# The six-expert part of a mixture-of-experts kernel: VectorE's and ScalarE's order written by hand, background work put into named slots

## Chip, core and metric

The kernel runs on one core of one Trainium2 chip. The metric is the device time of one execution in microseconds (us), taken as the median of several runs. TensorE multiplies matrices, VectorE (DVE in the profile) and ScalarE (ACT) do elementwise work, SyncE (SP) issues the transfers (DMA), GpSimd (POOL) has next to nothing to do here.

## The reference

A gated linear recurrence over 4 sequences of 768 positions gives `x` with 3072 rows (tokens) of 384 numbers. On it works a dense mixture of 8 experts, whose gate is normalised by 8 alternating row and column passes (Sinkhorn):

```python
P = np.exp(logits - logits.max())
for _ in range(8):
    P /= P.sum(1, keepdims=True) + 1e-09
    P /= P.sum(0, keepdims=True) + 1e-09
    P *= N / E
out = 0
for e in range(8):
    h = np.maximum(x @ w1[e], 0.0)      # 384 -> 1024
    out += P[:, e:e + 1] * (h @ w2[e])  # 1024 -> 384
```

Every expert is applied to every token, in float32.

## The kernel before

The first part computes the recurrence and, beside it, experts 0 and 1, whose outputs go to DRAM (`ye_d`). A short middle part (`phase2a`) loads the first tokens of the second part, prepares two sets of weights and does three of the eight normalisations. The rest is the six-expert part (`phase2b`), which the change concerns.

**Steps.** The tokens are four units of 768, taken two at a time (`su`, and `ul` within it). For each `su`, each expert `e` from 2 to 7, each of the two units and each of the four pairs `p` of 128-wide feature blocks there is a step: 96 steps, numbered `n` from 0. Within an expert's eight steps I write `q = 4*ul + p`. In n, an expert starts at 0, 8, 16, ..., the second pair of units at 48.

**Numbers.** Every float32 factor is split into a high and a low part, and a product takes three matmuls (high x high, high x low, low x high). "Hi" is a copy on ScalarE, "lo" a subtraction on VectorE.

**A step's first layer** computes a 2 x 2 grid of blocks (two feature blocks, two halves of 384 tokens) by Strassen's scheme with seven products P1 to P7 (`prod`, matmuls of lines 784 to 786) from weight sums S1 to S5 and token sums T1 to T4. P1, P6 and P7 have one term (3 matmuls each); P5, P2, P4 and P3 have two (6 each), as the third block of channels is added there. The products live in two PSUM banks (`psA`). ScalarE copies P1 to `s1` and P5 to `s5`; VectorE adds u2 = P6 + s1, u3 = P7 + u2, u4 = u2 + s5, c22 = u3 + s5, c11 = P2 + s1, c21 = P4 + u3, c12 = P3 + u4 (`add`, line 794). A product's bank is free when its copy or sum is done. `relu` then makes the hidden block's high half on ScalarE (line 805) and its low half on VectorE (line 806). With the product these are named h11, h00, h10, h01 for c22, c11, c21, c12.

**A step's second layer** works on the hidden blocks of the step before (`prev`): six groups of six matmuls, one for each tile of 128 tokens, `l2(0)` to `l2(5)` (here G0 to G5, `second`, lines 745 to 747). They gather over the four pairs of an expert in six PSUM banks. After the fourth pair VectorE adds the bank, weighted by the gate, to an accumulator `oa` in SBUF (line 754; for expert 2 ScalarE copies it, line 752), and after expert 7 the accumulator is written out.

**Background work** beside the steps:
- `raw_w` (line 647) loads raw weights; `prep_w` makes from them the five sums S1 to S5 (line 665) and, by ScalarE copies and VectorE subtractions (lines 667, 668), the tiles `wa`, `wb` (first layer) and `wc` (second layer). Twelve tiles of one expert fill the ring `wp`; the next expert's can be made only as these fall free.
- `load_x` (line 618) loads another unit's tokens; its jobs (lines 622 to 626) make T1 to T4.
- `rows` and `columns` do one normalisation of P.
- `start` (lines 729 to 733) loads the outputs of experts 0 and 1 for a tile, multiplies the accumulator by the gate and adds both.

**Order.** TensorE's order is written by hand: the build records its instructions in program order inside `tc.manual_schedule`. The order on VectorE, ScalarE and SP is found by the framework's scheduler when the kernel is built, from simulated times; each engine then runs its queue strictly in that order, and a DMA issue that waits holds the issues behind it on SP. In program order, background work stands in `l2` (two jobs a time), behind G1 and G4 (`rows`, `columns`), and behind G5 (`prep_w`, `start`). TensorE's order within a step is P1, P6, G0, P7, G1, P5, G2, P2, G3, P4, G4, P3, G5.

Of the kernel before, what the change touches and what calls it, by code (L numbers as in the profile page):

```python
# [13 lines left out]
H, D = 8, 48  # L14
# [40 lines left out]
class Net:  # L55
# [550 lines left out]
    def load_x(self, pool, ul, u):  # L606
        nc, V = self.nc, self.nc.vector
# [11 lines left out]
        jobs = []  # L619

        def job(o, a, b, op=ALU.subtract):
            jobs.append(lambda: V.tensor_tensor(o, a, b, op))

        def split(nm, r):
            jobs.append(lambda: nc.scalar.activation(X[nm][:, 0], r, AF.Copy))
            jobs.append(lambda: V.tensor_tensor(X[nm][:, 1], r, f(nm, 0), ALU.subtract))

        job(t[0], f("B11", 0), f("B11", 1), ALU.add)
        job(t[1], t[1], t[4], ALU.add)
        job(t[0], t[1], t[0])  # L630
        split("T1", t[0])
        job(t[2], f("B22", 0), f("B22", 1), ALU.add)
        job(t[3], t[2], t[0])
        split("T2", t[3])
        job(t[1], t[2], t[1])
        split("T3", t[1])
        job(t[2], f("B21", 0), f("B21", 1), ALU.add)
        job(t[2], t[2], t[3])
        split("T4", t[2])
        return jobs  # L640

    def raw_w(self):
        if self.nraw == len(self.todo):
            return
        e, p = self.todo[self.nraw]
        raw = self.wr.tile([128, 2, 2 * C], F32, tag="raw", name=f"raw{self.nraw}")
        self.nc.sync.dma_start(raw, self.w[e, 2 * p:2 * p + 2].rearrange("f p c -> p f c"))
        self.raw[self.nraw] = raw
        self.nraw += 1

    def prep_w(self):
        nc, V, A = self.nc, self.nc.vector, self.nc.scalar
        n = self.nprep
        if n == len(self.todo):
            return
        self.nprep += 1
        raw = self.raw.pop(n)
# [4 lines left out]
        w2 = self.wp.tile([128, 2, 2, C], F32R, tag="w", name=f"wc{n}")  # L662
        A11, A12, A13, A21, A22, A23 = (R[:, i, c] for i in range(2) for c in range(3))
        for o, a, b, op in ((0, A21, A22, ALU.add), (1, s[:, 0], A11, ALU.subtract), (2, A11, A21, ALU.subtract), (3, A12, s[:, 1], ALU.subtract), (4, A13, A23, ALU.subtract)):
            V.tensor_tensor(s[:, o], a, b, op)
        for t, k, src in ((wa, slice(0, 3), R[:, 0, :3]), (wa, slice(3, 5), R[:, 1, 1:3]), (wb, slice(0, 5), s), (w2, slice(0, 2), raw[:, :, C:])):
            A.activation(t[:, 0, k], src, AF.Copy)
            V.tensor_tensor(t[:, 1, k], src, t[:, 0, k].bitcast(F32), ALU.subtract)
        W = {nm: (wa, k) for k, nm in enumerate(("A11", "A12", "A13", "A22", "A23"))}
        W.update({f"S{k + 1}": (wb, k) for k in range(5)})  # L670
        self.W[n] = (W, w2)
        self.raw_w()

    def phase2a(self, c2):
# [8 lines left out]
        self.nraw = self.nprep = 0  # L683
# [14 lines left out]
        for k in range(HEAD):  # L698
            self.rows()
            more(3)  # L700
            self.columns(self.psK.tile([128, E], F32, tag="po", name=f"cp{k}"))
            if k == 1:
                self.raw_w()
                self.prep_w()
                self.prep_w()
# [3 lines left out]
    def phase2b(self, c2):  # L709
        tc, nc = self.tc, self.nc  # L710
        self.hp = c2.enter_context(tc.tile_pool(name="hp2", bufs=2))
        xb = c2.enter_context(tc.tile_pool(name="xb", bufs=1))
        psD = c2.enter_context(tc.tile_pool(name="psD", bufs=2, space=bass.MemoryType.PSUM))
        steps = [(su, e, ul, p) for su in range(SU) for e in range(2, E) for ul in range(SU) for p in range(NF // 2)]
        npair = NF // 2
        po, oa, H = {}, {}, {}
# [8 lines left out]
        def start(u, k):  # L725
            tt = tile_of(u, k)
            y = [self.wr.tile([128, C], F32, tag="y", name=f"y{q}_{tt}", bufs=4) for q in range(2)]
            for q in range(2):
                nc.sync.dma_start(y[q], self.ye_d[q][tt])
            o = oa[tt]  # L730
            nc.vector.tensor_scalar(o, o, self.P[:, tt, 2:3], None, ALU.mult)
            for q in range(2):
                nc.vector.scalar_tensor_tensor(o, y[q], self.P[:, tt, q:q + 1], o, ALU.mult, ALU.add)

        def second(st, k):
            su, e, ul, p = st
            u = su * SU + ul
            h, w2 = H[st]
            if p == 0:
# [8 lines left out]
            if p == npair - 1:  # L748
                tt = tile_of(u, k)
                if e == 2:  # L750
                    oa[tt] = self.xa.tile([128, C], F32, tag=f"oa{u % SU}_{k}", name=f"oa{tt}")
                    nc.scalar.activation(oa[tt], po[k], AF.Copy)
                else:
                    nc.vector.scalar_tensor_tensor(oa[tt], po[k], self.P[:, tt, e:e + 1], oa[tt], ALU.mult, ALU.add)
                if e == E - 1:
                    nc.sync.dma_start(self.out[tt * CH:tt * CH + CH, :], oa[tt])

        V, A = nc.vector, nc.scalar
        jobs, free = [], [(pool, tag) for pool, tag in ((self.psC, "po0"), (self.psC, "po1"), (self.psC, "po2"), (psD, "po"), (psD, "po"))]
        it = HEAD  # L760
        for n, st in enumerate(steps + [None]):
            prev = steps[n - 1] if n else None
            if st is None:
                for k in range(2 * NS):
                    second(prev, k)
                break
            su, e, ul, p = st
            u = su * SU + ul
            if e == 2 and ul == 0 and p == 1:
                jobs = self.load_x(xb, 1, u + 1)  # L770
            if e == E - 1 and ul == 1 and p == 1 and su + 1 < SU:
                jobs = self.load_x(self.xa, 0, u + 1)
            W, w2 = self.W[(su * (E - 2) + e - 2) * npair + p]
            X = self.X[u]
            h = {}
            H[st] = (h, w2)

            def prod(nm, *terms):
                pool, tag = free.pop(0) if n == 0 and nm not in ("P1", "P6") else (self.psA, "ph")
                ps = pool.tile([128, TH], F32, tag=tag, name=f"{nm}_{n}")  # L780
                for q, (wn, xn) in enumerate(terms):
                    (t, k), x = W[wn], X[xn]
                    first, last = q == 0, q == len(terms) - 1
# [18 lines left out]
            def relu(i, j, c):  # L802
                hh = self.hp.tile([128, TH], F32R, tag=f"hh{i}{j}", name=f"hh{i}{j}_{n}")
                hl = self.hp.tile([128, TH], F32R, tag=f"hl{i}{j}", name=f"hl{i}{j}_{n}")
                A.activation(hh, c, AF.Relu)  # L805
# [3 lines left out]
            def l2(k):  # L809
                if prev is not None:  # L810
                    second(prev, k)
                if p > 1 or n == 0 or su and e == 2:
                    for _ in range(min(2, len(jobs))):
                        jobs.pop(0)()
                if k == 1 and 0 < n <= ITERS - it:
                    self.rows()
                if k == 4 and 0 < n <= ITERS - it:
                    self.columns(self.psA.tile([128, E], F32, tag="ph", name=f"cp{it + n - 1}"))

            s1 = copy("s1", prod("P1", ("A11", "B11")))  # L820
            u2 = add("u2", prod("P6", ("S2", "T2")), s1)
            l2(0)
            u3 = add("u3", prod("P7", ("S3", "T3")), u2)
            l2(1)
# [19 lines left out]
            if e == 3:  # L844
                a = p * 2 if ul == 0 else 8 + p
                for k in range(a, a + 2 - ul):
                    start(su * SU + k // (2 * NS), k % (2 * NS))
# [174 lines left out]
```

## Time and profile before

| | |
|---|---|
| median of 3 runs | 1842.44 us (1840.32 to 1843.8) |
| span of the profiled execution, first to last instruction | 1839.6 us |
| six-expert part in it, P1 of step 0 to the last group's last matmul | 663.6 to 1833.7 us |
| TensorE, its weight loads, VectorE, ScalarE busy | 96%, 94%, 74%, 40% of the span |
| TensorE's granted clock, mean over the span | 0.988 |

The profiled execution has no time other than its span; what a run's time has beyond it lies ahead of the first and behind the last instruction. In the profile, PE is TensorE's matmul row and PEld the weight loads that run ahead of it. Matmuls overlap in their records (each of 384 columns is given 0.334 us, and the next starts 0.173 later), so a busy PE is not a sign of peak speed; a gap between starts, and what ended it, is what to read. A row of waits gives the waiting engine, its tile and line, the engine and line that released it, and then the total, the count and the longest in us. A row of groups gives line, engine, operation, tiles and shapes, the count, busy us and mean ns of one, and the idle time before them. A row by stretches gives the stretch, its length, then busy us and count of PE, PEld, DVE, ACT and POOL, the clock, the DMA's share and GB/s.

### The profile page before, as it was taken

The numbers are of one execution on the slowest core, as the hardware profiler recorded it, in microseconds if no ns is written. First come the engines' busy times: TensorE is split into PE (matmuls) and PEld (weight loads), VectorE is DVE, ScalarE is ACT, GpSimd is POOL, SyncE is SP. The second block draws the span as 40 slices with busy tenths as digits, with TensorE's granted clock in tenths as the row PEclk, the third lists the DMA queues.
The fourth block names the chain that finished last, engine by engine and source line by source line (L and its number), as shares of the span: only waits on it lengthen the run. The fifth ranks groups of instructions, "written<-read, shape, count | busy, mean of one in ns | idle before, by whom it ended". The sixth has DMA issues, their size and how long they took to land.

```text
span 1839.6 us, 30590 instructions
## 1 busy us (share of the span) xinstructions
PE 1774.3 (96%) x12024; PEld 1731.9 (94%) x12024; DVE 1361.8 (74%) x3060; ACT 734.3 (40%) x1597; POOL 6.4 (0%) x15
## 2 busy tenths in 40 slices
PE   5979999999999999999999999999999999999998
PEld 3869999999999989899999999998999999999998
DVE  7888989888883586967676767687776767575754
ACT  7534444445443443424242424343433333242421
POOL 1000000000000000000000000000000000000000
PEclk9979999999999999999999999999999999999999
DMA  6333433333332430401010101123220101020100
GB/s 209 96 104 88 132 113 110 116 111 111 118 97 73 147 112 4 150 20 52 18 52 18 52 18 52 49 96 97 69 86 18 52 5 65 1 69 1 52 24 31
DMA packets 120632, 132.83 MB, mean 72 GB/s; under 512 B 9632, under 2 KB 100512, under 8 KB 120480
## 3 DMA queue, kind: packets, MB, share of 16 engines
q1 hardware_dynamic: 119680, 130.41, 23.0%
q8 instruction: 96, 1.57, 0.4%
q14 instruction: 56, 0.46, 0.1%
q10 hardware_dynamic: 800, 0.39, 0.1%
HBM read 88.22 MB, written 23.59 MB: 61 GB/s over the span
## 4 chain that ended last, share of the span: by engine, by line
PE 82%; DVE 9%; DMA 4%; ACT 2%; issue 1%; SPq 1%; DVEq 0%; ACTq 0%
PE po L747 10%; PE po L745 10%; PE po L746 10%; PE P L784 9%; PE P L785 9%; PE P L786 9%; PE po L158 3%; PE ph L180 3%; PE ph L181 3%; PE ph L179 3%; PE po L160 3%; PE po L159 3%; PE sp L474 2%; PE y L491 2%; DMA raw<-in_w_dram 2%; PE U L469 1%
## 5 line engine op out<-in xcount | busy, mean ns | idle before, releaser
L747 PE MATMUL po<-wc,hl 128*128 128x384 f32 x1152 | 385.3, 334 | 3.1 <-DVE hl L806 3.1
L745 PE MATMUL po<-wc,hh 128*128 128x384 f32 x1152 | 385.0, 334 | 0.0
L746 PE MATMUL po<-wc,hh 128*128 128x384 f32 x1152 | 384.8, 334 | 0.0
L805 ACT ACTIVATE hh<-c 128x384 fp32r<-128x384 f32 x384 | 200.9, 524 | 322.2 <-DVE c L794 320.9
L806 DVE SCALAR_TENSOR_TENSOR hl<-c,hh 128x384 fp32r<-128x384 f32 x384 | 211.9, 552 | 66.5 <-ACT hh L805 58.5
L747 PEld LDWEIGHTS po<-wc,hl 128*128 128x128 f32 x1152 | 216.2, 188 | 4.4 <-DVE hl L806 4.4
L745 PEld LDWEIGHTS po<-wc,hh 128*128 128x128 f32 x1152 | 216.2, 188 | 0.4 <-ACT hh L805 0.4
L746 PEld LDWEIGHTS po<-wc,hh 128*128 128x128 f32 x1152 | 216.2, 188 | 0.0
L799 ACT ACTIVATE s<-P 128x384 f32<-128x384 f32 x192 | 94.1, 490 | 270.8 <-PE P L786 270.8
L185 ACT ACTIVATE hh<-ph 128x256 fp32r<-128x256 f32 x192 | 73.3, 382 | 243.7 <-PE ph L181 243.0
L180 PE MATMUL ph<-xl,w 128*128 128x256 f32 x576 | 162.8, 283 | 5.4 <-DVE xl L531 5.4
L179 PE MATMUL ph<-xh,w 128*128 128x256 f32 x576 | 162.2, 282 | 0.6 <-ACT xh L530 0.6
L181 PE MATMUL ph<-xh,w 128*128 128x256 f32 x576 | 162.4, 282 | 0.0
L784 PE MATMUL P<-B,wa 128*128 128x384 f32 x480 | 160.7, 335 | 0.9 <-DVE c L794 0.6
L786 PE MATMUL P<-B,wa 128*128 128x384 f32 x480 | 160.4, 334 | 0.0
L785 PE MATMUL P<-B,wa 128*128 128x384 f32 x480 | 160.4, 334 | 0.0
L158 PE MATMUL po<-w,hh 128*128 128x384 f32 x384 | 141.2, 368 | 1.2 <-ACT yst L163 1.2
L160 PE MATMUL po<-w,hl 128*128 128x384 f32 x384 | 130.7, 340 | 0.0
L159 PE MATMUL po<-w,hh 128*128 128x384 f32 x384 | 130.3, 339 | 0.0
L794 DVE TENSOR_TENSOR c<-P,u 128x384 f32<-128x384 f32 x192 | 106.2, 553 | 31.2 <-PE P L786 29.9
L794 DVE TENSOR_TENSOR u<-u,s 128x384 f32<-128x384 f32 x96 | 53.3, 555 | 100.9 <-ACT s L799 100.9
L187 DVE TENSOR_TENSOR hl<-hf,hh 128x256 fp32r<-128x256 f32 x192 | 80.4, 419 | 48.1 <-ACT hf L186 47.3
(188 smaller groups left out, 3665.4 us busy)
## 6 DMA issues: line engine op xcount, KB each, us to landing
raw<-in_w_dram SPq DMA_DIRECT2D x48, 768.0 KB, 4.3
qs<-z SPq DMA_DIRECT2D x144, 64.5 KB, 2.6
qk<-in_aqk_dram SPq DMA_DIRECT2D x12, 768.0 KB, 4.9
ks<-kh SPq DMA_DIRECT2D x144, 64.0 KB, 2.6
ye_d<-yst SPq DMA_DIRECT2D x48, 192.0 KB, 2.1
y<-ye_d SPq DMA_DIRECT2D x48, 192.0 KB, 2.4
z<-in_aqk_dram SPq DMA_DIRECT2D x11, 768.0 KB, 7.0
B<-x_d SPq DMA_DIRECT2D x40, 192.0 KB, 3.6
```

The lines of the kernel that those rows point to most:

```text
L158: nc.tensor.matmul(po[k], hh[:, s], w2h, start=f == 0, stop=False)
L179: nc.tensor.matmul(ph, w[:, 0, cs], xh[:, ct, :], start=(ct == 0), stop=False)
L180: nc.tensor.matmul(ph, w[:, 0, cs], xl[:, ct, :], start=False, stop=False)
L181: nc.tensor.matmul(ph, w[:, 1, cs], xh[:, ct, :], start=False, stop=(ct == NCT - 1))
L745: nc.tensor.matmul(po[k], hh[:, s], w2[:, 0, i], start=first, stop=False)
L746: nc.tensor.matmul(po[k], hh[:, s], w2[:, 1, i], start=False, stop=False)
L747: nc.tensor.matmul(po[k], hl[:, s], w2[:, 0, i], start=False, stop=last)
L784: nc.tensor.matmul(ps, t[:, 0, k], x[:, 0], start=first, stop=False)
L785: nc.tensor.matmul(ps, t[:, 0, k], x[:, 1], start=False, stop=False)
L786: nc.tensor.matmul(ps, t[:, 1, k], x[:, 0], start=False, stop=last)
L805: A.activation(hh, c, AF.Relu)
L806: V.scalar_tensor_tensor(hl, c, 0.0, hh.bitcast(F32), ALU.max, ALU.subtract)
```

## The change

1. **VectorE and ScalarE** in the six-expert part also get their order by hand: it is the program's order, inside `tc.manual_schedule`.
2. **Products and groups** alternate anew: P1, G0, P6, G1, P7, G2, P5, G3, P2, P4, G4, P3, G5.
3. **Background work** goes to named slots: slot 0 behind s1, slot 1 behind G1, slot 2 behind G2 (ahead of s5), slot 3 behind G4, slot 4 behind c12, slot 5 behind G5; `post[0]` (ScalarE) behind slot 0, `post[1]` behind h10's low half.
4. **Weights**: a raw load becomes two, first-layer and second-layer halves, with a buffer each; preparing is cut into `prep_w1` (steps q = 1, 5, 6, 7 and step 2) and `prep_w2` (q = 0, 6, 7, 1 and step 2). The two preparations behind step 0 become one each in steps 1 and 2.
5. **Normalisations** four to eight move from steps 1 to 5 to steps 4 to 8.
6. **Token jobs** (twelve for a unit, in a new order) go to steps 2 and 3, to q = 5, 6, 7 of expert 7, and to q = 2, 3 of the next pair's expert 2.
7. **Outputs of experts 0 and 1** are mixed in at q = 2, 3 of experts 3, 4 and 5, their loads issued a step earlier. The accumulator's first multiplication leaves VectorE: for the first two units ScalarE does it (six in q = 2 and six in q = 3 of expert 3), for the others it is the scale of expert 2's copy.

```diff
-    def raw_w(self):
-        raw = self.wr.tile([128, 2, 2 * C], F32, tag="raw", ...)
-        self.nc.sync.dma_start(raw, self.w[e, 2 * p:2 * p + 2].rearrange("f p c -> p f c"))
+    def raw_w(self, j):
+        src = self.w[e, 2 * p:2 * p + 2].rearrange("f p c -> p f c")
+        r = self.raw[j, n] = self.wr.tile([128, 2, C], F32, tag=f"raw{j}", name=f"raw{j}_{n}")
+        self.nc.sync.dma_start(r, src[:, :, j * C:j * C + C])
...
+            for k in range(2 * NS):
+                out(k)                      # if done: slots[(2, 2, 2, 3, 4, 5)[k]] gets evict(prev, k)
+            w2 = q in (0, 6, 7) and n > 0
+            w1 = q in (1, 5, 6, 7) or n == 2
+            if w2 and n > npair and self.nprep[1] < self.nprep[0]:
+                hi, lo = self.prep_w2()
+                post[0].append(hi)
+                slots[1].append(lo)
+            if w1 and self.nprep[0] < len(self.todo):
+                sums, his, los = self.prep_w1()
+                slots[0].append(sums)
+                post[0].extend([his[2], his[0], his[1]])
+                slots[2].extend([los[2], los[0], los[1]])   # los[1] ends with raw_w(0)
+                if q in (1, 2):
+                    hi, lo = self.prep_w2()
+                    post[1].append(hi)
+                    slots[3].append(lo)                     # ends with raw_w(1)
+            if n in sink:                                   # n = 4 .. 8
+                slots[2].append(self.rows)
+            if su == 0 and n == 2 or su and e == 2 and ul == 0 and p == 2:
+                slots[2].append(lambda: deal(3))
+            if e == 2 and ul == 0 and p == 3:
+                ...                                         # deal 2, 1, 4, 1, 1 in slots 0 to 4
+            if su and e == 2 and ul == 0 and p == 2:
+                ...                                         # deal 1 in slots 1 and 3
+            if e == E - 1 and q >= 5:
+                ...                                         # deal 1, 2, 1 in slots 3 to 5
+            if su == 0 and e == 3 and q in (2, 3):
+                ...                                         # six ScalarE scalings into post[0]
+            if 3 <= e < 6 and q in (1, 2):
+                ...                                         # fetch: y loads of two tiles
+            if 3 <= e < 6 and q in (2, 3):
+                ...                                         # mixin: one tile in slot 2, one in slot 4
...
             s1 = copy("s1", prod("P1", ("A11", "B11")))
+            fill(0)
+            for g in post[0]:
+                g()
+            l2(0)
             u2 = add("u2", prod("P6", ("S2", "T2")), s1)
-            l2(0)
+            l2(1)
+            fill(1)
             u3 = add("u3", prod("P7", ("S3", "T3")), u2)
-            l2(1)
+            l2(2)
+            fill(2)
             s5 = copy("s5", prod("P5", ("S1", "T1"), ("A23", "B32")))
             u4 = add("u4", u2, s5)
             c22 = add("c22", u3, s5)
-            l2(2)
+            h11 = high(1, 1, c22)
+            l2(3)
             c11 = add("c11", prod("P2", ("A12", "B21"), ("A13", "B31")), s1)
-            relu(1, 1, c22)
-            relu(0, 0, c11)
-            l2(3)
+            h00 = high(0, 0, c11)
+            low(1, 1, c22, h11)
             c21 = add("c21", prod("P4", ("A22", "T4"), ("A23", "B31")), u3)
-            relu(1, 0, c21)
+            h10 = high(1, 0, c21)
+            low(0, 0, c11, h00)
+            low(1, 0, c21, h10)
+            for g in post[1]:
+                g()
             l2(4)
+            if n in sink:
+                self.columns(self.psA.tile([128, E], F32, tag="ph", name=f"cp{n}"))
+            fill(3)
             c12 = add("c12", prod("P3", ("S4", "B22"), ("S5", "B32")), u4)
-            relu(0, 1, c12)
+            h01 = high(0, 1, c12)
+            fill(4)
+            low(0, 1, c12, h01)
             l2(5)
-            if n == 0:
-                self.prep_w()
-                self.prep_w()
-            if prev is not None and prev[2] == SU - 1:
-                self.prep_w()
-            ...                             # start() at expert 3
+            fill(5)
+        with tc.manual_schedule(engines={mybir.EngineType.DVE, mybir.EngineType.Activation}):
+            for n, st in enumerate(steps):
+                ...
+                step(n, st, steps[n - 1] if n else None)
```

More of the change, by code (lines that the diff above doesn't have):

```diff
@@ L651, in prep_w, with tt, hi, lo @@
-    def prep_w(self):
-        nc, V, A = self.nc, self.nc.vector, self.nc.scalar
-        n = self.nprep
+        def tt(o, a, b, op=ALU.subtract):
+            return lambda: V.tensor_tensor(o, a, b, op)
+        def hi(nm, r):
+            return lambda: A.activation(X[nm][:, 0], r, AF.Copy)
+        def lo(nm, r):
+            return lambda: V.tensor_tensor(X[nm][:, 1], r, f(nm, 0), ALU.subtract)
+        def both(*fs):
+            def run():
+                for g in fs:
+                    g()
+            return run
@@ new lines, in load_x @@
+        return [
+            tt(t[0], f("B11", 0), f("B11", 1), ALU.add),
+            tt(t[1], t[1], t[4], ALU.add),
+            both(tt(t[0], t[1], t[0]), hi("T1", t[0])),
+            tt(t[2], f("B22", 0), f("B22", 1), ALU.add),
+            both(tt(t[3], t[2], t[0]), hi("T2", t[3])),
+            lo("T1", t[0]),
+            both(tt(t[1], t[2], t[1]), hi("T3", t[1])),
+            lo("T2", t[3]),
+            tt(t[2], f("B21", 0), f("B21", 1), ALU.add),
+            both(tt(t[2], t[2], t[3]), hi("T4", t[2])),
+            lo("T3", t[1]),
+            lo("T4", t[2]),
+        ]
@@ L661, in prep_w @@
         wb = self.wp.tile([128, 2, 5, 128], F32R, tag="w", name=f"wb{n}")
[L662 to L668, printed above, removed]
@@ new lines, in hi, with lo, run, prep_w2 @@
+        def hi(q):
+            t, k, src = parts[q]
+            return lambda: A.activation(t[:, 0, k], src, AF.Copy)
+        def lo(q):
+            t, k, src = parts[q]
+            def run():
+                V.tensor_tensor(t[:, 1, k], src, t[:, 0, k].bitcast(F32), ALU.subtract)
+                if q == 1:
+                    self.raw_w(0)
+            return run
+        return sums, [hi(q) for q in range(3)], [lo(q) for q in range(3)]
+    def prep_w2(self):
+        V, A = self.nc.vector, self.nc.scalar
+        n = self.nprep[1]
+        self.nprep[1] += 1
+        raw = self.raw.pop((1, n))
+        w2 = self.wp.tile([128, 2, 2, C], F32R, tag="w", name=f"wc{n}")
+        self.W[n][1] = w2
+        def lo():
+            V.tensor_tensor(w2[:, 1], raw, w2[:, 0].bitcast(F32), ALU.subtract)
+            self.raw_w(1)
+        return lambda: A.activation(w2[:, 0], raw, AF.Copy), lo
@@ L674, in phase2a, with prep_w @@
+    def prep_w(self):
+        sums, his, los = self.prep_w1()
+        sums()
+        for q in (2, 0, 1):
+            his[q]()
+        for q in (2, 0, 1):
+            los[q]()
+        for g in self.prep_w2():
+            g()
     def phase2a(self, c2):
@@ L713, in phase2b @@
         psD = c2.enter_context(tc.tile_pool(name="psD", bufs=2, space=bass.MemoryType.PSUM))
-        steps = [(su, e, ul, p) for su in range(SU) for e in range(2, E) for ul in range(SU) for p in range(NF // 2)]
         npair = NF // 2
-        po, oa, H = {}, {}, {}
+        NE = E - 2
+        steps = [(su, e, ul, p) for su in range(SU) for e in range(2, E) for ul in range(SU) for p in range(npair)]
+        po, oa, H, Y, jobs = {}, {}, {}, {}, []
+        free = [(pool, tag) for pool, tag in ((self.psC, "po0"), (self.psC, "po1"), (self.psC, "po2"), (psD, "po"), (psD, "po"))]
+        sink = range(npair, npair + ITERS - HEAD)
         def acc(e, u, k):
@@ L723, in tile_of, with fetch, mixin @@
             return (NS * u + k % NS) * NCH + k // NS
-        def start(u, k):
+        def fetch(u, k):
             tt = tile_of(u, k)
-            y = [self.wr.tile([128, C], F32, tag="y", name=f"y{q}_{tt}", bufs=4) for q in range(2)]
+            Y[tt] = [self.wr.tile([128, C], F32, tag="y", name=f"y{q}_{tt}", bufs=4) for q in range(2)]
             for q in range(2):
-                nc.sync.dma_start(y[q], self.ye_d[q][tt])
-            o = oa[tt]
-            nc.vector.tensor_scalar(o, o, self.P[:, tt, 2:3], None, ALU.mult)
+                nc.sync.dma_start(Y[tt][q], self.ye_d[q][tt])
+        def mixin(u, k):
+            tt = tile_of(u, k)
+            o, y = oa[tt], Y.pop(tt)
             for q in range(2):
-                nc.vector.scalar_tensor_tensor(o, y[q], self.P[:, tt, q:q + 1], o, ALU.mult, ALU.add)
+                V.scalar_tensor_tensor(o, y[q], self.P[:, tt, q:q + 1], o, ALU.mult, ALU.add)
         def second(st, k):
@@ L758, in phase2b, with evict @@
[L758 to L766, printed above, removed]
+        def evict(st, k):
             su, e, ul, p = st
             u = su * SU + ul
[L769 to L774, printed above, removed]
-            h = {}
-            H[st] = (h, w2)
+            tt = tile_of(u, k)
+            if e == 2:
+                oa[tt] = self.xa.tile([128, C], F32, tag=f"oa{u % SU}_{k}", name=f"oa{tt}")
+                if u < SU:
+                    A.activation(oa[tt], po[k], AF.Copy)
+                else:
+                    A.activation(oa[tt], po[k], AF.Copy, scale=self.P[:, tt, 2:3])
+            else:
+                V.scalar_tensor_tensor(oa[tt], po[k], self.P[:, tt, e:e + 1], oa[tt], ALU.mult, ALU.add)
+            if e == E - 1:
+                nc.sync.dma_start(self.out[tt * CH:tt * CH + CH, :], oa[tt])
@@ new lines, in deal, with step, out, fill @@
+        def deal(k):
+            for _ in range(min(k, len(jobs))):
+                jobs.pop(0)()
+        def step(n, st, prev):
+            su, e, ul, p = st
+            u = su * SU + ul
+            q = ul * npair + p
+            done = prev is not None and prev[3] == npair - 1
+            h = {}
+            H[st] = (h, self.W[(su * NE + e - 2) * npair + p])
+            W, X = H[st][1][0], self.X[u]
+            slots = {k: [] for k in range(6)}
+            post = {k: [] for k in range(3)}
+            def out(k):
+                if done:
+                    slots[(2, 2, 2, 3, 4, 5)[k]].append(lambda: evict(prev, k))
+            for k in range(2 * NS):
[7 more added lines that the diff above has]
+            if w1 and self.nprep[0] < len(self.todo):
+                sums, his, los = self.prep_w1()
+                slots[0].append(sums)
[10 more added lines that the diff above has]
+            if e == 2 and ul == 0 and p == 3:
+                slots[0].append(lambda: deal(2))
+                slots[1].append(lambda: deal(1))
+                slots[2].append(lambda: deal(4))
+                slots[3].append(lambda: deal(1))
+                slots[4].append(lambda: deal(1))
+            if su and e == 2 and ul == 0 and p == 2:
+                slots[1].append(lambda: deal(1))
+                slots[3].append(lambda: deal(1))
+            if e == E - 1 and q >= 5:
+                slots[3].append(lambda: deal(1))
+                slots[4].append(lambda: deal(2))
+                slots[5].append(lambda: deal(1))
+            tiles = [(su * SU + k // (2 * NS), k % (2 * NS)) for k in range(4 * NS)]
+            if su == 0 and e == 3 and q in (2, 3):
+                for k in range(2 * NS):
+                    tt = tile_of(q - 2, k)
+                    post[0].append(lambda o=oa[tt], tt=tt: A.activation(o, o, AF.Copy, scale=self.P[:, tt, 2:3]))
+            if 3 <= e < 6 and q in (1, 2):
+                k = (e - 3) * 4 + (q - 1) * 2
+                fetch(*tiles[k])
+                fetch(*tiles[k + 1])
+            if 3 <= e < 6 and q in (2, 3):
+                k = (e - 3) * 4 + (q - 2) * 2
+                slots[2].append(lambda: mixin(*tiles[k]))
+                slots[4].append(lambda: mixin(*tiles[k + 1]))
+            def fill(k):
+                for g in slots[k]:
+                    g()
@@ L780, in prod @@
                 ps = pool.tile([128, TH], F32, tag=tag, name=f"{nm}_{n}")
-                for q, (wn, xn) in enumerate(terms):
+                for i, (wn, xn) in enumerate(terms):
                     (t, k), x = W[wn], X[xn]
-                    first, last = q == 0, q == len(terms) - 1
+                    first, last = i == 0, i == len(terms) - 1
                     nc.tensor.matmul(ps, t[:, 0, k], x[:, 0], start=first, stop=False)
@@ L800, in copy, with high, low @@
                 return o
[L802 removed]
+            def high(i, j, c):
                 hh = self.hp.tile([128, TH], F32R, tag=f"hh{i}{j}", name=f"hh{i}{j}_{n}")
+                A.activation(hh, c, AF.Relu)
+                return hh
+            def low(i, j, c, hh):
                 hl = self.hp.tile([128, TH], F32R, tag=f"hl{i}{j}", name=f"hl{i}{j}_{n}")
[L805 removed]
                 V.scalar_tensor_tensor(hl, c, 0.0, hh.bitcast(F32), ALU.max, ALU.subtract)
@@ L811, in l2 @@
                     second(prev, k)
[L812 to L818, printed above, removed]
             s1 = copy("s1", prod("P1", ("A11", "B11")))
+            fill(0)
+            for g in post[0]:
+                g()
+            l2(0)
             u2 = add("u2", prod("P6", ("S2", "T2")), s1)
-            l2(0)
+            l2(1)
+            fill(1)
             u3 = add("u3", prod("P7", ("S3", "T3")), u2)
-            l2(1)
+            l2(2)
+            fill(2)
             s5 = copy("s5", prod("P5", ("S1", "T1"), ("A23", "B32")))
```

74 lines of the change are left out of this document (29 added, 45 removed).

## Prediction

> **What bounds the kernel now.** I read the page's head first, then the time by stretches of whole steps, then what TensorE waited for, then the timeline at one wait.
>
> ```profile
> span 1839.6 us, 30590 instructions
> PE 1774.3 (96%) x12024; PEld 1731.9 (94%) x12024; DVE 1361.8 (74%) x3060; ACT 734.3 (40%) x1597; POOL 6.4 (0%) x15
> ```
>
> TensorE is nearly always busy, VectorE (DVE) three quarters, ScalarE (ACT) two fifths. Only time in which TensorE stands still can be won, since the change removes no matmul. The six-expert part has 96 steps; step 0 has only its 33 product matmuls, every other one 69. The stretches below are step 1; 2 to 5; 6 to 9; 10 to 44; 45 to 47; 48 to 57; 58 to 95. The first number behind the colon is the stretch's length.
>
> ```profile
> 669.36:686.38 17.02, 13.57 (x72) 12.05 (x72) 15.19 (x38) 6.51 (x14) 0.00 (x0) 1.00 0.47 139
> 686.38:735.13 48.75, 48.75 (x285) 48.75 (x285) 33.97 (x84) 17.03 (x35) 0.00 (x0) 1.00 0.01 2
> 735.13:787.82 52.69, 49.52 (x277) 47.59 (x277) 49.33 (x113) 21.02 (x43) 0.00 (x0) 1.00 0.47 149
> 787.82:1206.43 418.61, 418.61 (x2416) 418.58 (x2416) 284.78 (x584) 145.08 (x277) 0.00 (x0) 1.00 0.12 38
> 1206.43:1244.68 38.25, 36.57 (x209) 35.79 (x208) 31.99 (x68) 16.84 (x33) 0.00 (x0) 1.00 0.27 87
> 1244.68:1373.01 128.33, 122.16 (x691) 119.26 (x691) 99.42 (x214) 49.18 (x96) 0.00 (x0) 1.00 0.28 87
> 1373.01:1827.59 454.58, 454.58 (x2624) 454.43 (x2623) 302.11 (x611) 153.67 (x293) 0.00 (x0) 1.00 0.09 29
> ```
>
> The fourth row is the yardstick: 35 steps without a wait take 418.61, so a step takes 11.96 us and a matmul 0.1733 us, which I call p. Against 11.96 per step the rows exceed by 5.06, 0.91, 4.85, 0, 2.37, 8.73 and 0.10: 22.0 us in all, and all but the last 0.10 of it falls in 22 of the 95 steps, where the background work (weights, tokens, earlier experts' outputs, P's normalisation) crowds. The other 73 are at TensorE's pace. What TensorE's weight loads waited for in this part:
>
> ```profile
> PEld P L784 <- DVE c L794: 9.5, 9, 1.6
> PEld po L747 <- DVE hl L806: 4.4, 4, 1.5
> PEld P L784 <- ACT s L799: 4.3, 4, 1.5
> PEld P L784 <- DVE u L794: 2.0, 3, 1.0
> ```
>
> These make 20.2 of the 22.0. The waits are for a PSUM bank (a product's first matmul, L784, waits until the sum or copy that read the bank's last product is done) and for a hidden layer's low half (L747). No DMA is among them. One of them, at step 45:
>
> ```profile
> 1205.61 0.88 DVE L668 TENSOR_TENSOR wa<-raw,wa 128x384 fp32r<-128x384 f32 x2
> 1206.41 0.61 DVE L754 SCALAR_TENSOR_TENSOR oa<-po,P,oa 128x384 f32<-128x384 f32 x1
> 1206.94 0.55 DVE L806 SCALAR_TENSOR_TENSOR hl<-c,hh 128x384 fp32r<-128x384 f32 x1
> 1207.41 0.55 DVE L794 TENSOR_TENSOR c<-P,u 128x384 f32<-128x384 f32 x1
> ```
>
> ```profile
> 1206.78 0.34 PE L786 MATMUL P<-B,wa 128*128 128x384 f32 x1
> 1208.01 0.44 PE L784 MATMUL P<-T,wb 128*128 128x384 f32 x1 [0.90 <-DVE c L794]
> ```
>
> VectorE did weights and an output (L668, L754), which nobody waited for, ahead of the sum c12, which held P6's bank. P6 started at 1208.01, 0.05 after that sum's end. So the loss is one of order, and order is what changes.
>
> **The change: rooms between products.** Consumers take this long:
>
> ```profile
> 1003.62 0.33 PE L784 MATMUL P<-T,wb 128*128 128x384 f32 x1
> 1003.82 0.49 ACT L799 ACTIVATE s<-P 128x384 f32<-128x384 f32 x1 [0.44 <-PE P L786]
> ```
>
> ```profile
> 1008.57 0.56 DVE L794 TENSOR_TENSOR u<-u,s 128x384 f32<-128x384 f32 x1 [1.00 <-ACT s L799]
> 1009.04 0.55 DVE L794 TENSOR_TENSOR c<-u,s 128x384 f32<-128x384 f32 x1
> ```
>
> A reader starts 0.20 us after its product's end (the next product's start, 1003.62, to 1003.82). VectorE's neighbours start 0.47 apart though each lasts 0.55, so a chain of them is counted at duration less 0.08. In units of p from a step's start, the new TensorE order is P1 0-3, G0 to 9, P6 to 12, G1 to 18, P7 to 21, G2 to 27, P5 to 33, G3 to 39, P2 to 45, P4 to 51, G4 to 57, P3 to 63, G5 to 69. With two banks in turn, a product may start when the product before last has been read. Room for that read, before and after: P6 (waits for c12) 9p and 15p, that is 1.56 and 2.60 us; P7 (s1) 1.56 and 2.60; P5 (u2) 2.60 both; P2 (u3) 3.12 both; P4 (s5) 3.12 and 2.08; P3 (c11) 3.12 and 2.08; next P1 (c21) 3.12 both. G0's last low half comes 29p and 26p behind P4. So the two tightest rooms, where most waits lay, gain 1.04 each, and P4 and P3 lose 1.04.
>
> **The step's chain without background.** s1 is done at 1.21 us (0.52 + 0.20 + 0.49); u2 runs 2.28-2.83; u3 3.84-4.39; s5 5.92-6.41; u4 from 6.44, c22 from 6.91 to 7.46; c11 8.00-8.55, due at 57p = 9.88; c21 9.04-9.59, due 11.96; the low half of h10 done by 10.7, due 13.3; c12 11.12-11.67, due in the next step's 9p, 13.52; its high half 12.2 and low half 12.8. s5 is due at 45p = 7.80. The slack is thus 1.39 at s5, 1.33 at c11, 1.85 at c12.
>
> **What the named slots hold.**
>
> ```profile
> L799 ACT ACTIVATE s<-P 128x384 f32<-128x384 f32 x192 | 94.1, 490 | 270.8 <-PE P L786 270.8
> L805 ACT ACTIVATE hh<-c 128x384 fp32r<-128x384 f32 x384 | 200.9, 524 | 322.2 <-DVE c L794 320.9
> L667 ACT ACTIVATE wa<-raw 128x384 fp32r<-128x384 f32 x45 | 23.7, 526 | 80.1 <-DMA raw<-in_w_dram 71.5 <-PE P L786 8.5
> ```
>
> ```profile
> L754 DVE SCALAR_TENSOR_TENSOR oa<-po,P,oa 128x384 f32<-128x384 f32 x120 | 73.5, 612 | 16.3 <-PE po L747 16.1
> L668 DVE TENSOR_TENSOR wc<-raw,wc 128x768 fp32r<-128x768 f32 x46 | 44.0, 956 | 11.6 <-ACT wc L667 11.6
> L668 DVE TENSOR_TENSOR wb<-sum,wb 128x640 fp32r<-128x640 f32 x46 | 37.6, 816 | 0.0
> L665 DVE TENSOR_TENSOR sum<-raw 128x128 f32<-128x128 f32 x135 | 33.6, 285 | 39.0 <-DMA raw<-in_w_dram 39.0
> L668 DVE TENSOR_TENSOR wa<-raw,wa 128x384 fp32r<-128x384 f32 x45 | 24.8, 551 | 0.0
> L668 DVE TENSOR_TENSOR wa<-raw,wa 128x256 fp32r<-128x256 f32 x46 | 19.2, 417 | 0.0
> L596 DVE TENSOR_REDUCE cs<-P 128x8 f32<-128x192 f32 x6 | 3.1, 514 | 0.2
> ```
>
> - Slot 0, between the last low half (done 12.8 - 11.96 = 0.9) and u2's need: five weight sums, 5 x 0.285 = 1.4, end at 2.3. Covered; if not, u2 has until 4.68.
> - Slot 1: w2's low half, 0.88, from 2.75 to 3.6; u3 comes at 3.84. Covered.
> - Slot 2, from 4.31 to u4's 6.44, 2.1 us: three low halves 0.73 + 0.47 + 0.34 = 1.54, or three outputs 3 x 0.53 = 1.6. Covered. With `rows` behind the low halves (steps 5 to 7): five instructions, at most 5 x 0.514 = 2.6, at least half that. At the bound u4 starts at 8.45 and c11 ends at 9.94 against 9.88; at half, 1.3 earlier. I take nothing, and up to 0.5 us in all for the range.
> - Slots 3 to 5: single outputs or token jobs around c12, 0.5 to 1 us each, against c12's 1.85.
> - The twelve ScalarE scalings replace VectorE's; six of them behind s1, at 0.49 to 0.53 (s, wa rows; no row has this form), end at 1.21 + 3.2 = 4.4, ahead of s5's 5.92. VectorE loses 24 multiplications; off the path.
>
> **Where I expect new waits.** Step 2 alone has three low halves and then three token jobs in slot 2, the third with T1's high copy on ScalarE, which stands ahead of s5: 4.31 + 1.54 + 0.47 + 0.47 + 0.55 + 0.03 = 7.37, copy 0.53, s5 7.90-8.39, due 7.80: 0.6 lost, and 0.1 in refilling. Step 3 has four jobs there, no weights: its s5 ends by 7.3. Step 1, now free of the two weight preparations that stood in step 0: low10 of step 0 just meets G0; 0.2 lost. Five `columns` matmuls between G4 and P3 cost what they did in steps 2 to 5, 0.91 / 4 = 0.23 each: 1.15.
>
> **Transfers and SP's queue.**
>
> ```profile
> raw<-in_w_dram SPq DMA_DIRECT2D x48, 768.0 KB, 4.3
> wr<-in_w_dram SPq DMA_DIRECT2D x12, 384.0 KB, 3.9
> out_dram<-oa SPq DMA_DIRECT2D x24, 192.0 KB, 1.9
> ```
>
> ```profile
> tx<-x_d SPq DMA_DIRECT2D x4, 192.0 KB, 2.9
> ```
>
> ```profile
> DMA to landing us min/median/max: 4.0/4.3/6.6
> ```
>
> The raw weights come in 96 halves. A half's landing is bounded by 3.9 (a 384 KB row) and 6.6 (the worst whole); I take 4.3. Issued behind slot 2's low halves at 5.9 us, it lands at 10.2; slot 0 of the next step wants it at 12.9. The Trainium skill, "DMA: Bandwidth & Descriptors", § Anatomy of one DMA, speaks against halves: a fixed cost of about 2 us for each transfer, whatever its size (stated for transfers that GpSimd issues; these are SP's). The trace agrees in kind (3.9 for half of what takes 4.3); by the page or by the row, the half lands inside the 7.0 us from issue to need, and the sum is the same. Token loads at an expert's end: o of tile 4 is evicted in slot 4 of step 44 (near 12 us), out 1.9, load 2.9, so at 17 us; its job stands in slot 4 of step 45, 23 us. SP's queue may hold a weight load behind them for the same 5 us; covered. Output mixing (L733) now follows its y loads by a step.
>
> **Sum.** 22.0 won, less 0.2, 0.7 and 1.15, less 0.5 for small stumbles: 19.5. The profiled span of 1839.6 is 2.8 below the median of the runs, 1842.44, and I hold that distance: 1820.1 + 2.8 = 1822.9, say 1823.
>
> **The rivals.**
> A. The waits move to P4 and P3, whose rooms shrank. For: slot 2's work stands in a fixed order before u4, c22 and c11 now, and nothing can overtake it; a row of this trace for that order does not exist. Against: 1.3 us of slack by the rows. It decides once slot 2 exceeds 2.1 + 1.3 = 3.4 us. If the 48 steps that prepare weights each lost 0.2, that is 9.6: 1832.5. The Trainium skill, "Perfetto Trace Analysis", § Optimization Strategy, would name such a repeated gap a want of PSUM buffers.
> B. Slower: late weight halves. In the fixed order a sum that waits for its half holds u2, so P5, so everything. Sums may start as late as 11.96 + 4.68 - 0.55 - 1.4 = 14.7, so this decides at a landing of 8.8 us behind an issue at 5.9; the worst seen is 6.6. Before, such waits stood on VectorE 39.0 us in total without harm (sum row). If the halves queued behind token, y and output traffic and landed at 10.0, 1.2 in each of some 24 steps with a preparation just before: 29, less 19.5 won: 1852.
> C. No change: the crowding itself, not its order, is the limit. VectorE was busy 49.33 of 52.69 us in steps 6 to 9. For: total work hardly falls. Against: the work now also uses steps in which VectorE is a third idle (284.78 busy of 418.61 in the fourth row). With all 22.0 kept, the time is the old one, 1842.
>
> **Chances.** Forecast (1819.5 to 1827) 0.68, A 0.17, C 0.05, B and its like 0.10. A difference under 0.2% (3.7 us) can't be told from none here. A ends mostly below 1838.8, so faster 0.86, same 0.05, slower 0.09. Range: below stands the whole 22.0 and 0.9 more, 1819.5; above I take in more than half of A, 1834.
>
> **What would show it.** Right: every step but 1 to 9 at 11.96; no PE wait for c or hl at steps 45 to 57; step 2 some 0.7 long, by s. Wrong: PE waits at L784-like lines for s5 or c11 in weight steps (A); VectorE sums idle for raw with PE waiting for u (B); the same 22 us in the same steps (C).

## The result, and the profile after

The changed kernel takes 1823.08 us (median of 4 runs, 1821.37 to 1825.64) where the one before took 1841.53 (4 runs, 1840.32 to 1843.8): a ratio of 0.9894, 95% interval 0.9883 to 0.9906, so 18 us or 1.1% less. 1823 was forecast (how much of that is luck is said below). The profiled execution's span fell by 17.7, from 1839.6 to 1821.9.

The page's head and engine line of after:

```profile
span 1821.9 us, 30731 instructions
PE 1769.1 (97%) x12024; PEld 1733.5 (95%) x12024; DVE 1368.7 (75%) x3036; ACT 738.0 (41%) x1609; POOL 6.4 (0%) x15
```

VectorE lost its 24 multiplications (3060 to 3036 instructions), ScalarE got 12, and both are as busy as before. What changed is when they do it. What TensorE's weight loads waited for in the six-expert part, as shown of before:

```profile
PEld P L893 <- ACT s L908: 0.8, 1, 0.8
PEld P L893 <- DVE c L903: 0.7, 3, 0.2
PEld po L799 <- DVE hl L918: 0.2, 1, 0.2
```

Twenty waits of 20.2 us in those four rows have become five of 1.7. By stretches (step 1; 2; 3 and 4; 5 to 7; 8 to 95):

```profile
669.97:682.17 12.20, 12.20 (x70) 11.88 (x70) 10.59 (x24) 5.70 (x11) 0.00 (x0) 1.00 0.57 160
682.17:694.90 12.73, 12.24 (x70) 11.92 (x70) 9.98 (x23) 5.53 (x11) 0.00 (x0) 1.00 0.23 64
694.90:719.09 24.19, 24.19 (x142) 24.13 (x141) 19.21 (x42) 9.25 (x20) 0.00 (x0) 1.00 0.05 17
719.09:756.58 37.49, 37.06 (x214) 36.79 (x214) 33.13 (x86) 15.42 (x31) 0.00 (x0) 1.00 0.19 54
756.58:1809.29 1052.70, 1052.70 (x6075) 1052.70 (x6075) 756.66 (x1534) 379.64 (x732) 0.00 (x0) 1.00 0.16 47
```

The last row is the result: 88 steps in 1052.70, 11.96 each, and nothing beyond that but the 0.22 of the `columns` matmul in step 8. Everything that remains lies in steps 1 to 8. Against 11.96 a step the rows exceed by 0.24, 0.77, 0.27, 1.61 and 0.22: 3.1 in all, where it was 22.0. Of the 18.9 won, 0.6 went ahead of step 0, whose P1 starts at 664.2 and not at 663.6, and 0.6 behind the last group's last matmul.

The wait in step 2, on ScalarE and then on TensorE:

```profile
689.67 0.53 ACT L624 ACTIVATE T<-tx 128x384 fp32r<-128x384 f32 x1 [3.33 <-DVE tx L621]
690.10 0.47 ACT L908 ACTIVATE s<-P 128x384 f32<-128x384 f32 x1
```

```profile
690.63 0.45 PE L893 MATMUL P<-T,wa 128*128 128x384 f32 x1 [0.49 <-ACT s L908]
```

T1's copy stands ahead of s5, whose product had long ended; P4 waits for s5. From the step's start at 682.17 the copy begins at 7.50, s5 at 7.93, P4 at 8.46. The prediction had 7.37, 7.90 and 8.4. In step 5:

```profile
728.31 0.56 DVE L918 SCALAR_TENSOR_TENSOR hl<-c,hh 128x384 fp32r<-128x384 f32 x1
728.79 0.55 DVE L903 TENSOR_TENSOR c<-P,u 128x384 f32<-128x384 f32 x1
```

```profile
729.39 0.44 PE L893 MATMUL P<-B,wb 128*128 128x384 f32 x1
```

P3 starts 0.05 after the end of c21 (728.79 + 0.55), which stands behind h11's low half. This one was not forecast.

### The profile page after: what moved, and what is told of

It is laid out like the page before. It is cut to its first block, busy times and chain, and to the rows that moved or that the text cites. A ratio compares the mean times of both kernels' runs of the same rounds, so it can differ in the third digit from the quotient of the medians.

```text
span 1821.9 us, 30731 instructions
## 1 busy us (share of the span) xinstructions
PE 1769.1 (97%) x12024; PEld 1733.5 (95%) x12024; DVE 1368.7 (75%) x3036; ACT 738.0 (41%) x1609; POOL 6.4 (0%) x15
## 4 chain that ended last, share of the span: by engine, by line
PE 91%; DVE 5%; DMA 1%; ACT 1%; issue 1%; SPq 0%; DVEq 0%; ACTq 0%
PE po L799 11%; PE po L797 11%; PE po L798 11%; PE P L893 10%; PE P L894 10%; PE P L895 10%; PE po L158 4%; PE ph L180 4%; PE ph L181 3%; PE ph L179 3%; PE po L160 3%; PE po L159 3%; PE sp L474 2%; PE y L491 2%; PE U L469 1%
## 5 line engine op out<-in xcount | busy, mean ns | idle before, releaser
L180 PEld LDWEIGHTS ph<-xl,w 128*128 128x128 f32 x576 | 110.0, 191 | 8.2 <-DVE xl L531 8.2
```

Source lines behind the costliest of these rows:

```text
L180: nc.tensor.matmul(ph, w[:, 0, cs], xl[:, ct, :], start=False, stop=False)
```

## The experiments

Two theories stood against each other. The *order theory*: the gain comes from no background work standing ahead of a sum or copy that holds a PSUM bank. The *room theory*: it comes from the new alternation, which gives P6 and P7 1.04 us more. A third, the *load theory*, was about the halved weight loads. "Lost" below is the six-expert part's length from step 1 to 95 beyond 11.96 a step, as 22.0 before and 3.1 after: it leaves out the first 660 us, which differ from kernel to kernel (last section). All ratios are to the kernel before, measured beside each run. Where TensorE ran at half clock in these steps (last section), that is in "lost" too.

**The alternation alone.** In the kernel before:

```diff
             s1 = copy("s1", prod("P1", ("A11", "B11")))
+            l2(0)
             u2 = add("u2", prod("P6", ("S2", "T2")), s1)
-            l2(0)
+            l2(1)
             u3 = add("u3", prod("P7", ("S3", "T3")), u2)
-            l2(1)
+            l2(2)
...                                         # P5, l2(3), P2, P4, l2(4), P3, l2(5)
```

> The kernel before with nothing but the new alternation of products and groups on TensorE; VectorE and ScalarE are ordered by the scheduler as before. Order theory (the gain is that no background work stands ahead of a sum that holds a bank): the wider rooms of P6 and P7 swallow up to 1.04 us of each wait there, some 10 of the 13.8 us, and the waits for low halves and for u2 and most of step 1's 5 us stay: 1832 us (1828 to 1836). Room theory (the rooms of P6 and P7 are the gain): 1823 to 1826.

Measured: 1846.9 us, ratio 1.0017 (1.0004 to 1.003); 21.9 lost. TensorE's waits:

```profile
PEld po L747 <- DVE hl L806: 8.7, 10, 2.6
PEld P L784 <- DVE c L794: 7.0, 5, 3.4
PEld P L784 <- DVE u L794: 3.4, 5, 1.9
```

The waits for s are gone and those for c shrank from nine to five, but longer ones came for low halves and u. Neither theory's number was met. VectorE's order came out differently: in step 7, for one, u3 stood ahead of the weight sums before and stands behind them and two low halves here. So the run doesn't tell what the wider rooms bring under an unchanged order; alone, the alternation is worth nothing.

**Everything but the order by hand.** In the changed kernel:

```diff
-        with tc.manual_schedule(engines={mybir.EngineType.DVE, mybir.EngineType.Activation}):
+        if True:
```

> The changed kernel with VectorE's and ScalarE's order left to the scheduler; slots, alternation, halved loads and the rest stay, so the slots are only the program order. Order theory: the scheduler puts background ahead again and at least 5 us of waits return: 1828 to 1835. Room theory and the theory that the dealing out alone suffices: 1822 to 1825.

Measured: 1841.89, ratio 0.9996 (0.9985 to 1.0007), above the 1828 to 1835 of the order theory; 19.6 lost, of which three stretches at half clock are some 1.6 each. Slots, halves and alternation are all there and no time is gained. ScalarE and TensorE in step 9, which begins at 772.3:

```profile
774.62 3.13 ACT L873 ACTIVATE oa<-oa,P 128x384 f32<-128x384 f32 x6
777.65 0.47 ACT L908 ACTIVATE s<-P 128x384 f32<-128x384 f32 x1
```

```profile
778.17 0.44 PE L893 MATMUL P<-T,wb 128*128 128x384 f32 x1 [2.58 <-ACT s L908]
```

Six scalings of the accumulator, which in program order belong to steps 10 and 11, stand ahead of s1, whose product had ended at 772.8; P7, which needs P1's bank, waits for s1. VectorE in the same step likewise does eight output mixes of steps 10 and 11 ahead of u2, but P5 did not have to wait for that. In step 48 VectorE stood on a raw load, with u4, c22 and c11 queued behind it, and P3 waited for c11:

```profile
1255.56 0.69 DVE L677 TENSOR_TENSOR sum<-raw 128x128 f32<-128x128 f32 x3 [3.76 <-DMA raw<-in_w_dram]
```

```profile
1259.64 0.54 PE L893 MATMUL P<-B,wb 128*128 128x384 f32 x1 [2.20 <-DVE c L903]
```

So the scheduler puts background work ahead of copies and sums that hold a bank, on both engines, and the order by hand is what removes this.

**The old rooms.** In the changed kernel P6 and P7 go back ahead of G0 and G1 (P1, P6, G0, P7, G1, G2, P5, ...), VectorE's and ScalarE's order untouched:

```diff
-            l2(0)
             u2 = add("u2", prod("P6", ("S2", "T2")), s1)
-            l2(1)
+            l2(0)
             fill(1)
             u3 = add("u3", prod("P7", ("S3", "T3")), u2)
+            l2(1)
             l2(2)
```

> The changed kernel with P6 and P7 back at their old places (P1, P6, G0, P7, G1, G2, P5, and on as changed): their rooms are 1.56 us again, VectorE's and ScalarE's order is untouched. Order theory: c12 has 0.8 us of slack left, so only steps where it is late lose (the normalisation steps, steps with w2 in slot 3): 0 to 3 us, 1823 to 1826. Room theory: half of the gain or more goes, 1832 or more.

Measured: 1824.35, ratio 0.9897 (0.9876 to 0.9918), span 1822.0; 3.8 lost. With 1.56 us of room again the kernel keeps the gain, as the order theory had it; the room theory falls.

**The order by hand alone.** In the kernel before, nothing else changed:

```diff
+        with tc.manual_schedule(engines={mybir.EngineType.DVE, mybir.EngineType.Activation}):
             for n, st in enumerate(steps + [None]):
...                                         # the loop as before, further in
```

> The kernel before with VectorE's and ScalarE's order fixed to its own program order, nothing else. There a whole weight preparation (about 4.3 us of VectorE) stands behind a step's last low half (12.8 us), so u2 of the next step ends near 5.7 where the old alternation needs it at 3.64. Order theory: fixing an order is no gain in itself, what stands where is: 2 us lost in each of some 46 steps, 1900 to 1950 us. The theory that a fixed order alone is the gain: under 1835.

Measured: 1971.07 (one run), above the expected 1900 to 1950; 148.8 lost. In the plain steps behind a preparation, 22 to 24 for one, 1.97 to 1.99 each; other steps lost up to 6.3, step 1 14.8, and part of the loss is half clock, in twelve stretches. For the plain steps the size was right, the path not: the bank that came late was P1's, not P6's. ScalarE's copies of the weights wait there for VectorE's sums, and s1 stands behind them:

```profile
PEld P L785 <- ACT s L800: 108.3, 45, 12.6
```

An order by hand is as good as what stands in it.

**The price of a late load (rival B).** In the changed kernel a one-element read holds the raw half until slot 5:

```diff
-                if q == 1:
-                    self.raw_w(0)
...
+        def hold():
+            o = self.wr.tile([128, 1], F32, tag="hold", name=f"hold{n}")
+            V.tensor_copy(o, raw[:, 0, 0:1])
+            self.raw_w(0)
...
+                slots[5].append(hold)
```

> The changed kernel with the first-layer half of the raw weights held by a one-element read in slot 5, so that its next load is issued at about 12.9 us of a step and not at 5.9. By the chain worked out: landing near 17.0, sums then, u2 done near 6.9 of the next step where P5 needs it at 4.68: 2.1 to 2.4 us lost in each of 22 or 23 steps that follow a preparation, 1873 to 1880 us. If there is much more slack than worked out (or the transfers were never near): 1823 to 1830.

Measured: 1871.98 (one run); 47.4 lost. VectorE and TensorE in step 14, which begins at 843.0:

```profile
847.33 0.29 DVE L677 TENSOR_TENSOR sum<-raw 128x128 f32<-128x128 f32 x1 [3.37 <-DMA raw<-in_w_dram]
```

```profile
849.07 0.44 PE L898 MATMUL P<-T,wb 128*128 128x384 f32 x1 [1.20 <-DVE u L908]
```

The mechanism is the one described: sums late, u2 late, P5 late. The loss of a plain step is 1.3 to 1.6 and not 2.1 to 2.4, as a half lands sooner than I took:

```profile
DMA to landing us min/median/max: 3.0/3.2/4.9
```

That the time still comes near the expected 1873 to 1880 is luck: steps 2, 6, 7 and 47 lost 3.9 to 6.1 each, 18.6 together.

**The slack in slot 2 (rival A).** The three low halves of the weights twice, and three times:

```diff
-                V.tensor_tensor(t[:, 1, k], src, t[:, 0, k].bitcast(F32), ALU.subtract)
+                for _ in range(EXTRA[0] + 1):
+                    V.tensor_tensor(t[:, 1, k], src, t[:, 0, k].bitcast(F32), ALU.subtract)
...
+        EXTRA[0] = 1                        # at the start of phase2b; 2 in the other run
```

> The changed kernel with each of the three first-layer low halves of the weights done twice in slot 2 (the same values): 1.54 us more of VectorE there in 46 steps, 3.1 in all. The prediction put the point from which P3 waits for c11 at 3.4: ordinary steps lose nothing, the normalisation steps and the last of expert 7 some 2 to 4 us in all, 1825 to 1827. If the margin is smaller than worked out (rival A): 0.3 to 1 in every such step, 1838 to 1870.

> The same with the low halves three times: 4.6 us in slot 2, 1.2 beyond the point at 3.4. c11 ends at 10.4 against 9.88: 0.6 to 0.7 us lost in each of 46 steps, more where steps follow each other: 1850 to 1875 us. If the slack is far greater than worked out: under 1835.

Twice: 1835.91, ratio 0.9953 (0.9938 to 0.9968); 14.8 lost. Thrice: 1924.2 (one run); 101 lost. Twice, steps 10 to 45:

```profile
788.66:1219.22 430.56, 430.56 (x2486) 430.56 (x2485) 337.57 (x680) 152.23 (x295) 0.00 (x0) 1.00 0.18 51
```

That is 36 steps at 11.96: plain steps lose nothing, as expected, but the time is well above the expected 1825 to 1827. The miss is in the crowded steps: step 2 lost 3.4, steps 5 to 7 2.5 to 3.4 each, and I had put them at 2 to 4 together. VectorE in step 13, a plain one, begun at 824.54, with the halves twice:

```profile
828.85 1.67 DVE L689 TENSOR_TENSOR wb<-sum,wb 128x640 fp32r<-128x640 f32 x2
830.44 1.94 DVE L689 TENSOR_TENSOR wa<-raw,wa 128x384 fp32r<-128x384 f32 x4
832.30 0.55 DVE L906 TENSOR_TENSOR u<-u,s 128x384 f32<-128x384 f32 x1
832.77 0.55 DVE L906 TENSOR_TENSOR c<-u,s 128x384 f32<-128x384 f32 x1
833.24 0.55 DVE L906 TENSOR_TENSOR c<-P,s 128x384 f32<-128x384 f32 x1
```

The six took 3.45 us (828.85 to 832.30), and c11 ends at 9.25 of the step, 0.63 ahead of its due time 9.88. Thrice, in step 13, begun at 848.01:

```profile
852.33 2.53 DVE L689 TENSOR_TENSOR wb<-sum,wb 128x640 fp32r<-128x640 f32 x3
854.77 2.99 DVE L689 TENSOR_TENSOR wa<-raw,wa 128x384 fp32r<-128x384 f32 x6
857.68 0.55 DVE L906 TENSOR_TENSOR u<-u,s 128x384 f32<-128x384 f32 x1
858.15 0.55 DVE L906 TENSOR_TENSOR c<-u,s 128x384 f32<-128x384 f32 x1
858.62 0.55 DVE L906 TENSOR_TENSOR c<-P,s 128x384 f32<-128x384 f32 x1
```

```profile
859.23 0.44 PE L896 MATMUL P<-B,wb 128*128 128x384 f32 x1 [1.17 <-DVE c L906]
```

The nine took 5.35 us (852.33 to 857.68), not 4.6, since a repeat into the same tile does not overlap (last section). c11 then ends at 11.16 of the step, 1.28 late, and P3 waits for just that: 1.45 to 1.69 lost in a plain step that prepares weights, where 0.6 to 0.7 was expected. So the point from which P3 waits for c11 is 3.45 + 0.63 = 4.08 by the one run and 5.35 - 1.28 = 4.07 by the other, and not 3.4: there is 0.7 more slack than worked out.

**Whole loads.** In the changed kernel, with nine buffers instead of thirteen for s1 to c12 to make room:

```diff
+        if j == 1:
+            return
...
-        r = self.raw[j, n] = self.wr.tile([128, 2, C], F32, tag=f"raw{j}", name=f"raw{j}_{n}")
-        self.nc.sync.dma_start(r, src[:, :, j * C:j * C + C])
+        r = self.wr.tile([128, 2, 2 * C], F32, tag="raw", name=f"raw_{n}", bufs=2)
+        self.nc.sync.dma_start(r, src)
+        self.raw[0, n], self.raw[1, n] = r[:, :, :C], r[:, :, C:]
```

> The changed kernel with each pair's raw weights loaded by one transfer of 768 KB into one of two whole buffers, as the halves are used (room for it comes from 9 instead of 13 buffers for s1 to c12). Order theory: the load has 7 us from issue to need and lands in 4.3, so nothing changes: the same steps lose the same, 3.1 us in all, 1822 to 1825. Load theory (the halves are part of the gain): the steps behind a preparation lose 0.3 or more each, 1830 or more.

Measured: 1825.43, ratio 0.9899 (0.9882 to 0.9917); 3.1 lost, in the same steps (step 0 began 3.4 us later than in the changed kernel, which the time holds too). TensorE's waits are those of after:

```profile
PEld P L896 <- ACT s L911: 0.8, 1, 0.8
PEld P L896 <- DVE c L906: 0.7, 3, 0.2
PEld po L802 <- DVE hl L921: 0.2, 1, 0.2
```

The load theory falls: halving the loads is no part of the gain in time.

**Normalisations where they were.** In the changed kernel:

```diff
-        sink = range(npair, npair + ITERS - HEAD)
+        sink = range(1, 1 + ITERS - HEAD)
```

> The changed kernel with normalisations four to eight in steps 1 to 5, where they were before, and not in 4 to 8. By the chain: step 2 then has low halves, rows (1.8 us) and three token jobs ahead of T1's copy and s5: 0.8 + 1.8 = 2.6 lost; step 3 has rows and four jobs: T4's copy ends 0.5 to 1 past s5's due time, 1.0 to 1.5 lost; steps 1, 4 and 5 0.2 to 0.5 each. In all 4.5 to 5.5 instead of 3.1: 1825. If moving the normalisations were what freed steps 6 to 9: those stay free here too, and step 1 to 5 lose nothing: 1822.

Measured: 1827.8, ratio 0.9914 (0.9896 to 0.9931); 8.8 lost. Step 2's wait for s5 is 2.6 us long as expected, step 3 loses 2.1, step 1 1.5. Beyond the expectation of 4.5 to 5.5, TensorE ran at half clock behind step 2's wait, from 693.9 to 697.3 (last section), some 1.6 of the 8.8. So in this kernel moving the normalisations off the token jobs is worth 5.7 us. Steps 6 to 9 lose nothing here either, so it is not what freed them.

**A better version.** In the changed kernel:

```diff
-            low(1, 1, c22, h11)
             c21 = add("c21", prod("P4", ("A22", "T4"), ("A23", "B31")), u3)
             h10 = high(1, 0, c21)
+            low(1, 1, c22, h11)
...
-                slots[2].append(lambda: deal(3))
+                slots[2].append(lambda: deal(3 if su else 2))
+                slots[4].append(lambda: deal(0 if su else 1))
```

> The changed kernel with h11's low half put behind the sum c21 in VectorE's order, and in step 2 only two token jobs in slot 2, the third in slot 4. If the 0.3 us in each of steps 5 to 7 is P3 waiting for c21 behind that low half, and the 0.8 us in step 2 is s5 behind T1's copy, both go: 1.6 us, 1821.4. If they have another cause (the columns matmul itself, TensorE's queue), the steps stay at 12.5 and 12.7 us.

Measured: 1821.72 (5 runs, 1819.96 to 1824.14), ratio 0.9883 (0.9866 to 0.99), span 1819.8. Steps 1 to 7, and 8 to 95:

```profile
670.27:754.90 84.63, 84.63 (x492) 84.63 (x492) 71.88 (x173) 35.91 (x72) 0.00 (x0) 1.00 0.22 61
754.90:1807.60 1052.70, 1052.70 (x6075) 1052.70 (x6075) 748.13 (x1534) 379.66 (x732) 0.00 (x0) 1.00 0.16 47
```

1.1 lost, 0.23 at each of the five `columns` matmuls and nothing else: both causes are confirmed, and step 1's 0.25 went too, which I had not expected. It beats both kernels by its profile, the changed one by 2.0 us of this part; the interval of its ratio overlaps that of the changed kernel, so the times alone don't separate the two.

## Why the prediction was right, and where a step was off

- *The bound* (22.0 us of waits in 22 steps, by order and not by DMA): right. 18.9 of it went, 19.5 was forecast. That the time came out within 0.1 of 1823 is luck: the span was 1821.9 and not 1820.1, and the distance from the profiled span to the median, held at 2.8, was 1.2.
- *Rooms*: the tables of rooms and of the chain held, but I listed the wider rooms of P6 and P7 as if they carried the gain. They don't: without them 3.8 is lost instead of 3.1, and alone they bring nothing. The gain is the order by hand with the background dealt into it: the dealing without the order brings nothing (1841.89), the order without the dealing costs 126 us (1971.07 against 1845.12 beside it).
- *Step 2* (0.7, by s5 behind T1's copy): 0.77, by that. *Step 1* (0.2): 0.25. *`columns`* (five times 0.23): 1.15.
- *Slot 2 with `rows`* was the mis-sized term. I took half the bound of 2.6, and nothing lost. `rows` fills 1.76 us (741.86 to 743.62 in the run with the lows twice), and the wait did not come at c11, which I had checked, but at c21, which I had given its ordinary due time of 11.96: in these steps the `columns` matmul takes a bank in between, so that P3 needs c21 by 10.05 (58p). Three times 0.3, 0.9 in all, where 0.5 stood in the sum for all small stumbles.
- *Transfers*: hidden, as said; VectorE's wait for raw fell from 39.0 us in 35 waits to 2.2 in one. But 3.9 was no bound from below for a half: after shows 2.9, 3.1 and 4.0 (shortest, median, longest). The Trainium skill, "DMA: Bandwidth & Descriptors", § Anatomy of one DMA, has about 2 us plus size by 436 GB/s (stated for transfers that GpSimd issues), which for 384 KB is an estimate of 2.9; that agrees better than my row of another load did.
- *Rival A* did not come about: slot 2's ordinary 1.5 to 1.6 us stays far below its point. That point was mis-sized, 4.1 and not 3.4: I added c11's slack to slot 2's 2.1 and left out the 0.6 us between 7.38, when VectorE could follow c22, and 8.00, when P2's end lets c11 begin. My own chain for `rows` (1.54 + 2.6, c11 at 9.94 against 9.88) gives 4.1 too. *Rival B* is real at 1.4 us a step once a load is issued 7 us later; here it isn't. *Rival C* falls with the 88 steps at 11.96.

Not settled: why step 0 starts 0.6 later, which is well inside the scatter told of below; which of the scheduler's assumed durations is off; and how much each piece of the dealing carries, as only the normalisations were put back alone.

## What to carry to other kernels

Read a nearly saturated engine by stretches of equal work: a few stretches held all of the loss here, and the number that a clean stretch gives is both the yardstick and the floor. Then write down for each in-order engine the time at which every consumer is due and what stands ahead of it, transfers included; that table gave the residual waits of steps 1 and 2 to 0.1 us and missed those of steps 5 to 7, where a due time was taken over from an ordinary step. A slot's slack can be measured by doing its work twice. An automatic order made from simulated times, a good program order that it is free to change, and a fixed order with the work in lumps each failed by itself; the two parts had to be tried together to see it.

## What the runs showed of the hardware

- A gap in TensorE's work can cost more than itself. In the run without the order by hand, 2.9 us lay between the starts of two matmuls in step 9, and TensorE then ran at half clock for 3.4 us:

```profile
778.60:782.00 3.40, 3.40 (x13) 3.40 (x12) 2.12 (x5) 1.55 (x4) 0.00 (x0) 0.51 0.88 294
```

  Matmuls came 0.32 apart instead of 0.173, which is some 1.6 us more. In step 1 of the same run two gaps of 1.4 each, close together, did it as well, and so did one of 2.8 in step 2 with the normalisations where they were. A gap of 3.15 in step 2 with the lows twice did not, nor one of 3.4 in step 49 with the alternation alone, so a gap's length alone does not decide. The Trainium skill, "TensorE: Matmul & The Clock Gate", § What's actually happening, tells of a free-running window of 3.4 us and of the clock halved after an idle one. The length agrees, and a window that runs on its own would fit that longer gaps were spared; here gaps shorter than a window were enough.
- The first 660 us differ between kernels that have nearly the same program there: step 0 begins between 662.0 and 668.0 us, and the two latest, 667.7 and 668.0, have the most time at half clock ahead of it, 51 us against 41 to 44 for the others. One at 667.0 has 44, so that is not all of it.
- The same VectorE subtraction into the same tile again starts 0.85 after the one before for 640 elements, 0.03 after its end (1.67 for two, 2.53 for three), where different ones overlap by 0.08.
